# Turning gathered rows with DMA transposes of 16-bit planes in place of TensorE, in an FFT filter with a mixture of experts

## The chip, the cores and the metric

The kernel runs on one core of a Trainium2 chip. The metric is device time in microseconds (us) of one execution, the median of the runs shown. The engines are called as in the profile: PE (TensorE matmuls), PEld (its weight loads), DVE (VectorE), ACT (ScalarE), POOL (GpSimd) and SP (SyncE, which only issues DMAs here).

## The reference

A spectral filter over each of 8 sequences of 2496 rows of 256, then a mixture of 8 experts, each row going to the two experts with the highest noisy logits:

```python
X = np.fft.rfft(x, axis=1)
y = np.fft.irfft(X * (filt_r + 1j * filt_i)[None], n=2496, axis=1)
x = y.reshape(19968, 256)
logits = x @ w_gate
noisy = logits + np.log1p(np.exp(x @ w_noise)) * noise
top2 = np.argpartition(-noisy, 2, axis=1)[:, :2]      # then a softmax over the two: top2_w
out = np.zeros((19968, 256))
for e in range(8):
    for k in range(2):
        mask = top2[:, k] == e
        h = np.maximum(x[mask] @ w1[e], 0.0)           # w1[e] is 256 x 1024
        out[mask] += top2_w[mask, k, None] * (h @ w2[e])
```

## The kernel before

**Precision.** Every large product is made of three matmuls: each fp32 operand is split into a rounded high part (a cast on ACT, name ending in `h`) and the rest (a subtraction on DVE, ending in `l`), and `_mm3` adds high x high, low x high and high x low (L121 to L123).

**Two streams.** The FFT is a stream of small steps over the 8 sequences ("sets"): matrix products of 39 and 64 points, then the gate's logits and top two, then lists of rows for each expert, written to `lst`; the filtered rows with their gate values go to `y` in memory. The experts' stream works on blocks. A block is up to 512 rows of one expert: set 0 gives 2 blocks, set 1 ten; later sets give pairs of blocks of one expert (parts i = 0 and 1, which share the weights), the end has single blocks, then blocks of 256 and 128 rows. 71 blocks have 512 rows. `run` mixes the streams: after each of the 13 places of a block (`yield`) it takes as many FFT steps of later sets as `PACE` allows: the number of steps times the set's length in places may not exceed the places done times `PACE[i]`, 200 for the second set. In front of a weight change at a set's start `FILL` may add steps, and PE's instructions of the turn are then pinned behind them. The engines' orders come from a scheduler at build time; a pin (`after`, `pin`) fixes one instruction behind another.

**A block.** `fetch` keeps up to two blocks ahead. `gather` issues for each tile of 128 rows an indirect DMA from POOL (L993) into a slot of `stage` (8 slots `xg` of 264 columns: 256 values, 8 gates). `front` loads the expert's weights through SP (`load_w`, L1030) and splits them (`wsplit`, L1058, L1059). `turn` brings rows to columns: for each half `kc` of the 256 values four PE transposes of 128x128 (L1009) fill one PSUM bank `xps`, ACT casts it to `mxh` (L1013), DVE makes `mxl` (L1014); POOL copies the block's gate column to `gt` (L1018). Then, for each eighth f of the 1024 hidden values, six matmuls into an `hps` bank (of every three, two have the tag `hps` and the third shares `yps`), ACT's `hh` (relu, L1096) and DVE's `hl` (L1097), with w2's casts between where the weights are new. Last, for each of four row tiles t, eight times a 512-column and a 256-column matmul (L1121, L1122) into one of two `yps` banks, ACT's `o` (times the gate, L1126), DVE's sum of the second half (L1128), and POOL's indirect DMA that adds the rows to `out` (L1129). The next block's `turn` is called between h and y, so that the scheduler may place it beside the y matmuls.

Of the kernel before, what the change touches and what calls it, by code (L numbers as in the profile page):

```python
# [11 lines left out]
R32 = mybir.dt.float32r  # L12
F16 = mybir.dt.float16
I32 = mybir.dt.int32
AF = mybir.ActivationFunctionType
ALU = mybir.AluOpType
AX = mybir.AxisListType
# [5 lines left out]
NG = 22  # L23
# [103 lines left out]
    return ap.bitcast(F32)  # L127


PACE = {0: 110, 1: 200, 2: 40}  # L130
PACES = 115
FILL = {0: 0, 1: 14}
RAW = 3
# [8 lines left out]
class Moe:  # L142
# [39 lines left out]
    def setup(self):  # L182
# [12 lines left out]
        self.sgn = cp.tile([64, 20], F32, name="sgn")  # L195


        self.stage = cp.tile([128, 2048 + 8 * YW + 1536], F32, name="stage")
# [252 lines left out]
    def logits(self, r):  # L451
        nc, P = self.nc, self.P
        if r == 0:
            self.uh = P.tile([120, 24, 16], R32, name="uh")
# [262 lines left out]
    def gate(self, bt, lgp):  # L717
# [30 lines left out]

        m, c, oh = [], [], []
        for i in range(2):  # L750
            mi, ci, oi = t(f"m{i}", [RP, NG]), t(f"c{i}", [RP, NG]), t(f"oh{i}")
# [213 lines left out]
        nc.gpsimd.tensor_copy(ids, t)  # L965
        return ids, n, nt, s, self.tabs[i]

    def front(self, blk, xg, fill=None):


        nc = self.nc
        lt, n, nt, s, tabi, ready = blk
        with self.after(self.spw):
            re = nc.sync.value_load(tabi[0:1, 1, s:s + 1], min_val=0, max_val=E - 1)
        self.ra = nc.gpsimd.value_load(tabi[0:1, 1, s:s + 1], min_val=0, max_val=E - 1)
        w1st = self.load_w(re, "w1", nt)
        w1 = [self.wsplit(w1st[q], "w1", q) for q in range(4)]
        w2st = self.load_w(re, "w2", nt)
        if fill:
            fill()  # L980
        if fill and self.held_any:
            xT = self.pin(self.turn, xg, nt, hold=False, only=[self.nc.tensor.engine])
        else:
            xT = self.turn(xg, nt)
        return w1, xT, w2st

    def gather(self, blk, i):

        lt, n, nt, s, tabi, ready = blk
        xg = []  # L990
        for t in range(nt):
            x = self.slot("xg")
            self.pin(lambda: self.nc.gpsimd.indirect_dma_start(  # L993
                out=x, out_offset=None, in_=self.y[:BLK + ready * ROWS],
                in_offset=bass.IndirectOffsetOnAxis(ap=lt[:, i, t:t + 1], axis=0)),
                hold=False, only=[self.nc.gpsimd.engine])
            xg.append(x)
        return xg, self.turns["xg"] + 1 - nt

    def turn(self, xg, nt):  # L1000

        nc, P = self.nc, self.P
        xT = []
        xg, at = xg
        w = 128 * nt
        for kc in range(2):
            q = self.PS.tile([128, 512], F32, name="xps", bufs=1)
            for t in range(nt):
                nc.tensor.transpose(q[:, t * 128:(t + 1) * 128], xg[t][:, kc * 128:(kc + 1) * 128], self.ident)  # L1009
# [3 lines left out]
            nc.scalar.copy(h, q[:, :w])  # L1013
            nc.vector.tensor_sub(l, q[:, :w], f32v(h))  # L1014
            xT.append((h, l))
        gate = P.tile([128, 4, 1], F32, name="gt", bufs=3)[:, :nt]
        rows = self.stage[:, 2048:2048 + 8 * YW].rearrange("p (s w) -> p s w", w=YW)[:, at:at + nt, D:]
        nc.gpsimd.tensor_copy(gate, rows[:, :, bass.ds(self.ra, 1)])  # L1018
        xT.append(gate)
        return xT  # L1020

    def load_w(self, re, nm, nt):
# [39 lines left out]
    def fetch(self, may):  # L1062

        if len(self.ahead) < 2 and may():
            p = next(self.parts, None)
            if p is not None:
                self.ahead.append((*p, self.gather(*p)))

    def expert(self, parts, may, fill=None):

        nc, P = self.nc, self.P
        self.parts, self.ahead = parts, []
        self.fetch(lambda: True)
        cur = None
        while self.ahead:
            blk, i, xg = self.ahead.pop(0)
            lt, n, nt, s, tabi, ready = blk
            w = 128 * nt
            if cur is None:
                cur = self.front(blk, xg, fill)  # L1080
# [4 lines left out]
            self.fetch(may)  # L1085
            hh = []
            for f in range(8):

                p = self.PS.tile([128, 512], F32, name="hps", tag="hps" if f % 3 < 2 else "yps", bufs=2)[:, :w]
                for kc in range(2):  # L1090
                    wh, wl = w1[f // 2]
                    o = (f % 2) * 128
                    _mm3(nc, p, wh[:, kc, o:o + 128], wl[:, kc, o:o + 128], *xT[kc], start=(kc == 0), stop=(kc == 1))
                h = P.tile([128, 512], R32, name="hh", bufs=8)[:, :w]
                l = P.tile([128, 512], R32, name="hl", bufs=8)[:, :w]
                nc.scalar.activation(h, p, AF.Relu)  # L1096
                nc.vector.scalar_tensor_tensor(l, p, 0.0, f32v(h), op0=ALU.max, op1=ALU.subtract)  # L1097
                hh.append((h, l))
                if f % 2 and i == 0:
                    w2.append(self.wsplit(w2st[f // 2], "w2", f // 2))  # L1100
                yield
            late = not self.ahead
            if late:
                self.fetch(lambda: True)
            if self.ahead:
                b2, i2, x2 = self.ahead[0]
                cur = (w1, self.turn(x2, nt), None) if i2 else self.front(b2, x2, fill if late else None)
            self.fetch(may)
            yield
            for t in range(nt):  # L1110

# [14 lines left out]
                nc.scalar.activation(o, p, AF.Copy, scale=gate[:, t])  # L1126
                if wide:
                    nc.vector.scalar_tensor_tensor(o, bank[:, 1], gate[:, t], o, op0=ALU.mult, op1=ALU.add)  # L1128
                a = nc.gpsimd.indirect_dma_start(  # L1129
# [116 lines left out]
```

## Time and profile before

| | |
|---|---|
| median of 3 runs | 2316.27 us (2315.95 to 2317.04) |
| profiled execution | 2308.6 us, span 2306.8 us |
| PE busy | 2253.9 us, 98% |
| DVE busy | 1540.0 us, 67% |
| ACT busy | 1183.1 us, 51% |
| POOL busy | 925.5 us, 40% |
| mean granted TensorE clock | 0.993 of full speed |
| DMA | 328.58 MB, 142 GB/s over the span |

Busy time counts each engine alone. Matmuls overlap their neighbours in the records (a 512-column matmul is shown with 0.39 to 0.40 us while the next starts 0.23 us after it), so a PE near 100% says that PE did not wait. What an edit is worth is read from the waits, the chain that ended last, and the distance from one start to the next. The profiled execution is 7.7 us shorter than the median of the runs.

### The profile page before, as it was taken

The numbers are of one execution on the slowest core, as the hardware profiler recorded it, in microseconds if no ns is written. First come the engines' busy times: TensorE is split into PE (matmuls) and PEld (weight loads), VectorE is DVE, ScalarE is ACT, GpSimd is POOL, SyncE is SP. The second block draws the span as 40 slices with busy tenths as digits, with TensorE's granted clock in tenths as the row PEclk, the third lists the DMA queues.
The fourth block names the chain that finished last, engine by engine and source line by source line (L and its number), as shares of the span: only waits on it lengthen the run. The fifth ranks groups of instructions, "written<-read, shape, count | busy, mean of one in ns | idle before, by whom it ended". The sixth has DMA issues, their size and how long they took to land.

```text
span 2306.8 us, 39164 instructions
## 1 busy us (share of the span) xinstructions
PE 2253.9 (98%) x13023; PEld 1888.2 (82%) x13023; DVE 1540.0 (67%) x3348; ACT 1183.1 (51%) x2369; POOL 925.5 (40%) x819
## 2 busy tenths in 40 slices
PE   8889999999999999999999999999999999999998
PEld 5448888888788888888888888888888888889997
DVE  4767797687669765875659655964444445557886
ACT  6655655654554554444544444444344444546775
POOL 4014253343334333443344433435454544444442
PEclk9989999999999999999999999999999999999999
DMA  8686757755655555454544553444444444657774
GB/s 239 178 255 188 199 141 195 177 149 135 171 137 126 140 140 129 103 144 118 118 114 106 137 142 85 91 99 89 96 92 91 90 98 105 149 138 233 218 215 130
DMA packets 283957, 328.58 MB, mean 142 GB/s; under 512 B 37243, under 2 KB 196963, under 8 KB 283747
## 3 DMA queue, kind: packets, MB, share of 16 engines
q1 hardware_dynamic: 222435, 241.60, 34.5%
q0 software_dynamic: 61312, 84.40, 21.6%
q8 instruction: 104, 1.70, 0.3%
q14 instruction: 106, 0.87, 0.1%
HBM read 221.44 MB, written 105.25 MB: 142 GB/s over the span
## 4 chain that ended last, share of the span: by engine, by line
PE 89%; DMA 4%; DVE 3%; ACT 2%; issue 1%; SPq 1%; POOL 0%; POOLq 0%; ACTq 0%; DVEq 0%
PE yps L1121 21%; PE hps L121 12%; PE hps L122 12%; PE hps L123 12%; PE yps L1122 10%; PE xps L1009 3%; PE q L428 2%; PE yps L123 2%; PE yps L121 2%; PE yps L122 2%; PE q L492 1%; PE u L439 1%; DMA stage<-w 1%; DMA x<-x 1%; PE q L317 1%
## 5 line engine op out<-in xcount | busy, mean ns | idle before, releaser
L1121 PE MATMUL yps<-w,hh 128*128 128x512 f32 x2080 | 737.6, 399 | 0.6 <-DVE stage L1128 0.6
L1129 POOL DMA_INDIRECT out<-stage,ids x316 | 524.8, 1661 | 291.2 <-DVE stage L1128 116.9
L993 POOL DMA_INDIRECT stage<-y,ids x316 | 324.0, 1025 | 623.7 <-PE xps L1009 247.1
L1122 PE MATMUL yps<-w,hl 128*128 128x256 f32 x2080 | 563.3, 280 | 0.1
L1097 DVE SCALAR_TENSOR_TENSOR hl<-hps,hh 128x512 fp32r<-128x512 f32 (+2 forms) x712 | 435.0, 626 | 153.7 <-ACT hh L1096 151.9
L122 PE MATMUL hps<-mxl,w1h 128*128 128x512 f32 (+2 forms) x1424 | 533.0, 375 | 0.0
L121 PE MATMUL hps<-mxh,w1h 128*128 128x512 f32 (+2 forms) x1424 | 524.1, 378 | 1.7 <-DVE hl L1097 1.4
L123 PE MATMUL hps<-mxh,w1l 128*128 128x512 f32 (+2 forms) x1424 | 525.0, 370 | 0.0
L1096 ACT ACTIVATE hh<-hps 128x512 fp32r<-128x512 f32 (+2 forms) x712 | 377.7, 550 | 247.2 <-PE hps L123 241.7
L1121 PEld LDWEIGHTS yps<-w,hh 128*128 128x128 f32 x2080 | 384.2, 188 | 80.4 <-DVE stage L1128 0.9
L1122 PEld LDWEIGHTS yps<-w,hl 128*128 128x128 f32 x2080 | 391.1, 188 | 19.9 <-DVE mxl L1014 1.2
L121 PEld LDWEIGHTS hps<-mxh,w1h 128*128 128x128 f32 x1424 | 265.1, 188 | 50.5 <-DVE hl L1097 3.7
L123 PEld LDWEIGHTS hps<-mxh,w1l 128*128 128x128 f32 x1424 | 268.4, 188 | 45.5
L122 PEld LDWEIGHTS hps<-mxl,w1h 128*128 128x128 f32 x1424 | 268.3, 188 | 40.4 <-issue 0.2
L1126 ACT ACTIVATE stage<-yps,gt 128x256 f32<-128x256 f32 x316 | 142.3, 476 | 281.1 <-PE yps L1122 256.7
L1128 DVE SCALAR_TENSOR_TENSOR stage<-yps,gt,stage 128x256 f32<-128x256 f32 x260 | 119.4, 479 | 184.5 <-ACT stage L1126 184.1
L1014 DVE TENSOR_TENSOR mxl<-xps,mxh 128x512 fp32r<-128x512 f32 (+2 forms) x178 | 112.1, 630 | 149.1 <-ACT mxh L1013 147.0
L1013 ACT CAST mxh<-xps 128x512 fp32r<-128x512 f32 (+2 forms) x178 | 95.9, 539 | 203.3 <-PE xps L1009 170.3
L1058 ACT CAST w1h<-stage 128x512 fp32r<-128x512 f32 x180 | 111.8, 621 | 99.8 <-PE hps L122 52.1
L1059 DVE TENSOR_TENSOR w1l<-stage,w1h 128x512 fp32r<-128x512 f32 x180 | 123.7, 687 | 55.5 <-ACT w1h L1058 54.6
L965 POOL CAST ids<-lt 128x8 int32<-128x8 f32 (+3 forms) x63 | 16.2, 257 | 336.2 <-DMA lt<-lst 330.1
L1059 DVE TENSOR_TENSOR w<-stage,w 128x512 fp32r<-128x512 f32 x216 | 142.4, 686 | 7.9 <-ACT w L1058 7.4
(222 smaller groups left out, 3082.4 us busy)
## 6 DMA issues: line engine op xcount, KB each, us to landing
stage<-w SPq DMA_DIRECT2D x396, 256.0 KB
x<-x SPq DMA_DIRECT2D x88, 256.0 KB
fd<-c SPq DMA_DIRECT2D x77, 240.0 KB
wb<-w SPq DMA_DIRECT2D x18, 1024.0 KB
fx<-fd SPq DMA_DIRECT2D x140, 128.0 KB
out<-z SPq DMA_DIRECT2D x24, 702.0 KB
y<-yt SPq DMA_DIRECT2D x40, 248.6 KB
y<-yt SPq DMA_DIRECT2D x40, 234.0 KB
```

Of the source, the lines that this page charges most:

```text
L121: nc.tensor.matmul(o, lh, rh, start=start, stop=False)
L122: nc.tensor.matmul(o, lh, rl, start=False, stop=False)
L123: nc.tensor.matmul(o, ll, rh, start=False, stop=stop)
L993: self.pin(lambda: self.nc.gpsimd.indirect_dma_start(out=x, out_offset=None, in_=self.y[:BLK + ready * ROWS], in_offset=bass.IndirectOffse ...
L1059: nc.vector.tensor_sub(l, sv, f32v(h))
L1096: nc.scalar.activation(h, p, AF.Relu)
L1097: nc.vector.scalar_tensor_tensor(l, p, 0.0, f32v(h), op0=ALU.max, op1=ALU.subtract)
L1121: nc.tensor.matmul(bank, h, hl, start=(f == 0), stop=False)
L1122: nc.tensor.matmul(p, l, hl[:, 0], start=False, stop=(f == 7))
L1126: nc.scalar.activation(o, p, AF.Copy, scale=gate[:, t])
L1128: nc.vector.scalar_tensor_tensor(o, bank[:, 1], gate[:, t], o, op0=ALU.mult, op1=ALU.add)
L1129: a = nc.gpsimd.indirect_dma_start(out=self.io["out"][:BLK + ready * ROWS], out_offset=bass.IndirectOffsetOnAxis(ap=ids[:, t:t + 1], axis= ...
```

## The change

A block of 512 rows from the second set on (`by_dma`: 4 tiles and `ready` over 1) is turned without PE. For each two of its row tiles ACT copies the rows' fp32 values as 16-bit halves into two planes, all low halves and then all high halves of a row (`flip`, 128x1024 elements of 16 bits; the buffer `pl` has one slot for two tiles). SP then issues for each of the two tiles a DMA transpose of 128 x 512 16-bit values (128 KB) into `xt`, which has one buffer for a whole block. `turn` has DVE interleave the two planes of a half `kc` again into fp32 columns (128 x 1024 elements of 16 bits into `x32`, one slot), pinned behind the last `hl` of the block before; ACT's cast and DVE's subtraction read `x32` in SBUF instead of PSUM. 69 blocks go this way: 138 plane copies on ACT, 276 DMA transposes on SP, 138 copies on DVE, and 552 PE transposes fewer.

The first plane copy of a block is called in the h phase two turns ahead (after f = 4), the second after its predecessor's turn; both are pinned behind an activation. To make room, `xg` has 4 slots instead of 8 and `yo` 4 instead of 6. For such blocks the third bank of the h loop is `xps` (now free, one buffer) instead of `yps`. The gate copy is made when the planes are begun. `PACE` of the second set is 225. Two smaller tiles share buffers (`uh`, `oh`).

```diff
-PACE = {0: 110, 1: 200, 2: 40}
+PACE = {0: 110, 1: 225, 2: 40}
...
-        at, n, w = {"wst": (0, 4, 512), "xg": (2048, 8, YW), "yo": (2048 + 8 * YW, 6, 256)}[nm]
+        at, n, w = {"wst": (0, 4, 512), "xg": (2048, 4, YW), "yo": (2048 + 4 * YW, 4, 256),
+                    "x32": (3072 + 4 * YW, 1, 512), "pl": (3584 + 4 * YW, 1, 512)}[nm]
...
-        if fill and self.held_any:
-            xT = self.pin(self.turn, xg, nt, hold=False, only=[self.nc.tensor.engine])
+        if fill and self.held_any and ent[3] is None:
+            xT = self.pin(self.turn, ent, hold=False, only=[self.nc.tensor.engine])
...
+    def flip(self, late=None):
+
+        if self.turning is None:
+            ent = next((e for e in self.ahead if e[3] is None), None)
+            if self.standing or ent is None or not self.by_dma(ent[0]):
+                return
+            self.standing = True
+            xt = self.P.tile([128, 4, 512], U16, name="xt", bufs=1)
+            ent[3] = xt, self.take(ent)
+            self.turning, self.turned = ent, 0
+        ent, at = self.turning, self.turning[2][1]
+        xt, t = ent[3][0], self.turned
+        pl = self.slot("pl").bitcast(U16).rearrange("p (t two d) -> p t two d", t=2, two=2)
+        rows = self.held_rows(at + t, 2)[:, :, :D].bitcast(U16).rearrange("p t (d two) -> p t two d", two=2)
+        with self.after(late):
+            self.nc.scalar.copy(pl, rows)
+        for k in range(2):
+            self.nc.sync.dma_start_transpose(xt[:, :, 128 * (t + k):128 * (t + k) + 128], pl[:, k].rearrange("p two d -> p (two d)"))
+        self.turned += 2
+        if self.turned == 4:
+            self.turning = None
+
+    def by_dma(self, blk):
+        return blk[2] == BLK // 128 and blk[5] > 1
...
         for kc in range(2):
-            q = self.PS.tile([128, 512], F32, name="xps", bufs=1)
-            for t in range(nt):
-                nc.tensor.transpose(q[:, t * 128:(t + 1) * 128], xg[t][:, kc * 128:(kc + 1) * 128], self.ident)
+            if ent[3]:
+                q = self.slot("x32")
+                with self.after(self.lastl):
+                    nc.vector.tensor_copy(q.bitcast(U16).rearrange("p (t two) -> p two t", two=2), ent[3][0][:, kc::2])
+            else:
+                q = self.PS.tile([128, 512], F32, name="xps", bufs=1)
+                for t in range(nt):
+                    nc.tensor.transpose(q[:, t * 128:(t + 1) * 128], xg[t][:, kc * 128:(kc + 1) * 128], self.ident)
...
+            while self.turning or any(a[3] is None and self.by_dma(a[0]) for a in self.ahead):
+                self.flip(e)
+            if not self.ahead or self.by_dma(self.ahead[0][0]) or nt < BLK // 128:
+                self.fetch(may)
+            third = ("xps", 1) if ent[3] else ("yps", 2)
...
-                p = self.PS.tile([128, 512], F32, name="hps", tag="hps" if f % 3 < 2 else "yps", bufs=2)[:, :w]
+                tag, bufs = ("hps", 2) if f % 3 < 2 else third
+                p = self.PS.tile([128, 512], F32, name="hps", tag=tag, bufs=bufs)[:, :w]
...
+                if f == 4:
+                    self.flip(e)
                 yield
             late = not self.ahead
             if late:
                 self.fetch(lambda: True)
+                self.flip()
...
             self.fetch(may)
+            self.flip()
             yield
```

The order of the instructions moves with it. In the rows below a name is the tile written, an arrow, and the tiles read. First PE at the end of a block in the part of the program that has no FFT work left; `mxh_18925` is the next block, and the last h matmul of the block that ends stands 14 rows above the first one shown. Before:

```order
L1121 MATMUL yps<-w_18658,hh 128x512
L1122 MATMUL yps<-w_18658,hl 128x256
L1121 MATMUL yps<-w_18683,hh 128x512 x2
L1122 MATMUL yps<-w_18683,hl 128x256 x2
L121 MATMUL hps<-mxh_18925,w1h 128x512
L1009 MATMUL xps<-ident,stage 128x128 x4
L122 MATMUL hps<-mxl_18926,w1h 128x512
L123 MATMUL hps<-mxh_18925,w1l 128x512
```

After, from the last h matmul of a block (`mxh_19323`) on; `mxh_19556` is the next block:

```order
L124 MATMUL hps<-mxh_19323,w1l 128x512
L1180 MATMUL yps<-w_19527,hl 128x256 x2
L1179 MATMUL yps<-w_19527,hh 128x512 x2
L1180 MATMUL yps<-w_19527,hl 128x256 x2
L1179 MATMUL yps<-w_19552,hh 128x512 x2
L1180 MATMUL yps<-w_19552,hl 128x256 x2
L1179 MATMUL yps<-w_19552,hh 128x512 x2
L1180 MATMUL yps<-w_19552,hl 128x256 x2
L122 MATMUL hps<-mxh_19556,w1h 128x512 x3
L123 MATMUL hps<-mxl_19557,w1h 128x512
```

The transposes between the h and y matmuls are gone, and fourteen y matmuls of two row tiles stand between the last h matmul of one block and the first of the next, which opens three banks at once.

ACT at the same kind of place. Before, the casts of the next block (`mxh`) stand among the last activations of h (L1096), ahead of the y tiles' `o` (L1126):

```order
L1058 CAST w_20036<-stage 128x512
L1096 ACTIVATE hh<-hps 128x512 x5
L1013 CAST mxh_20044<-xps 128x512
L1096 ACTIVATE hh<-hps 128x512
L1013 CAST mxh_20053<-xps 128x512
L1126 ACTIVATE stage<-yps,gt 128x256 x2
```

After (L1030 is the plane copy, L1150 `hh`, L1061 `mxh`, L1184 `o`):

```order
L1150 ACTIVATE hh<-hps 128x512 x3
L1030 COPY stage<-stage 128x1024
L1150 ACTIVATE hh<-hps 128x512 x5
L1061 CAST mxh_19556<-stage 128x512
L1184 ACTIVATE stage<-yps,gt 128x256 x2
L1061 CAST mxh_19561<-stage 128x512
L1184 ACTIVATE stage<-yps,gt 128x256 x2
L1030 COPY stage<-stage 128x1024
L1150 ACTIVATE hh<-hps 128x512
```

The casts have moved behind the last activation of h, one plane copy stands inside the h phase, and the other between the last `o` and the next block's first `hh`.

DVE after, at the end of that block (L1151 is `hl`, L1053 the interleaving copy, L1062 `mxl`, L1186 the y tiles' sum):

```order
L1151 SCALAR_TENSOR_TENSOR hl<-hps,hh 128x512 x8
L1053 COPY stage<-xt 128x2x512
L1062 TENSOR_TENSOR mxl_19557<-stage,mxh_19556 128x512
L1186 SCALAR_TENSOR_TENSOR stage<-yps,gt,stage 128x256 x2
L1053 COPY stage<-xt 128x2x512
L1062 TENSOR_TENSOR mxl_19562<-stage,mxh_19561 128x512
```

Both copies stand behind all eight `hl` of the block before, the second behind the sums of its first two y tiles too.

More of the change, by code (lines that the diff above doesn't have):

```diff
@@ L14 @@
 I32 = mybir.dt.int32
+U16 = mybir.dt.uint16
 AF = mybir.ActivationFunctionType
@@ L195, in setup @@
         self.sgn = cp.tile([64, 20], F32, name="sgn")
-        self.stage = cp.tile([128, 2048 + 8 * YW + 1536], F32, name="stage")
+        self.stage = cp.tile([128, 2048 + 4 * YW + 2048], F32, name="stage")
         self.turns = {}
@@ L453, in logits @@
         if r == 0:
-            self.uh = P.tile([120, 24, 16], R32, name="uh")
+            self.uh = P.tile([120, 24, 16], R32, name="uh", tag="ut0", bufs=1)
             self.ul = P.tile([120, 24, 16], R32, name="ul")
@@ L750, in gate @@
         for i in range(2):
-            mi, ci, oi = t(f"m{i}", [RP, NG]), t(f"c{i}", [RP, NG]), t(f"oh{i}")
+            mi, ci = t(f"m{i}", [RP, NG]), t(f"c{i}", [RP, NG])
+            oi = P.tile(sh, F32, name=f"oh{i}", tag=("gl", "oh1")[i], bufs=1)
             v.tensor_reduce(mi, nz, axis=AX.X, op=ALU.max)
@@ L980, in front @@
             fill()
-        if fill and self.held_any:
-            xT = self.pin(self.turn, xg, nt, hold=False, only=[self.nc.tensor.engine])
+        if fill and self.held_any and ent[3] is None:
+            xT = self.pin(self.turn, ent, hold=False, only=[self.nc.tensor.engine])
         else:
-            xT = self.turn(xg, nt)
+            xT = self.turn(ent)
         return w1, xT, w2st
     def gather(self, blk, i):
+        nc = self.nc
         lt, n, nt, s, tabi, ready = blk
+        if i == 0:
+            self.ra = nc.gpsimd.value_load(tabi[0:1, 1, s:s + 1], min_val=0, max_val=E - 1)
         xg = []
@@ L992, in gather @@
             x = self.slot("xg")
-            self.pin(lambda: self.nc.gpsimd.indirect_dma_start(
+            self.pin(lambda: nc.gpsimd.indirect_dma_start(
                 out=x, out_offset=None, in_=self.y[:BLK + ready * ROWS],
                 in_offset=bass.IndirectOffsetOnAxis(ap=lt[:, i, t:t + 1], axis=0)),
-                hold=False, only=[self.nc.gpsimd.engine])
+                hold=False, only=[nc.gpsimd.engine])
             xg.append(x)
-        return xg, self.turns["xg"] + 1 - nt
@@ L1000, in turn, with held_rows, take @@
-    def turn(self, xg, nt):
+        return xg, self.turns["xg"] + 1 - nt, self.ra
+    def held_rows(self, at, n):
+        return self.stage[:, 2048:2048 + 4 * YW].rearrange("p (s w) -> p s w", w=YW)[:, at:at + n]
+    def take(self, ent):
+        xg, at, ra = ent[2]
+        gate = self.P.tile([128, 4, 1], F32, name="gt", bufs=3)[:, :len(xg)]
+        self.nc.gpsimd.tensor_copy(gate, self.held_rows(at, len(xg))[:, :, D:][:, :, bass.ds(ra, 1)])
+        return gate
+    def flip(self, late=None):
[18 more added lines that the diff above has]
+            self.turning = None
@@ L1015, in turn @@
             xT.append((h, l))
[L1016 to L1019, printed above, removed]
+        self.standing = self.standing and ent[3] is None
+        xT.append(ent[3][1] if ent[3] else self.take(ent))
+        ent[3] = ent[3] or ()
         return xT
@@ L1066, in fetch @@
             if p is not None:
-                self.ahead.append((*p, self.gather(*p)))
+                self.ahead.append([*p, self.gather(*p), None])
     def expert(self, parts, may, fill=None):
         nc, P = self.nc, self.P
-        self.parts, self.ahead = parts, []
+        self.parts, self.ahead, self.turning, self.standing, self.lastl = parts, [], None, False, None
         self.fetch(lambda: True)
+        self.flip()
         cur = None
         while self.ahead:
-            blk, i, xg = self.ahead.pop(0)
+            ent = self.ahead.pop(0)
+            blk, i = ent[:2]
             lt, n, nt, s, tabi, ready = blk
@@ L1079, in expert @@
             if cur is None:
-                cur = self.front(blk, xg, fill)
+                cur = self.front(ent, fill)
             w1, xT, w2st = cur
@@ L1104, in expert @@
                 self.fetch(lambda: True)
+                self.flip()
             if self.ahead:
-                b2, i2, x2 = self.ahead[0]
-                cur = (w1, self.turn(x2, nt), None) if i2 else self.front(b2, x2, fill if late else None)
+                e2 = self.ahead[0]
+                cur = (w1, self.turn(e2), None) if e2[1] else self.front(e2, fill if late else None)
             self.fetch(may)
+            self.flip()
             yield
```

17 lines of the change are left out of this document (9 added, 8 removed).

## The prediction

> **What bounds the kernel now.** I read the page first (busy shares, then the chain of waits), next the busy time in windows of 100 us, then the groups of instructions with their shapes apart, and last the timeline at one turn of a block and the DMA and wait lists.
>
> From the page of the kernel before, the busy shares, the DMA queue of SP, and the chain by engine and by line:
>
> ```profile
> PE 2253.9 (98%) x13023; PEld 1888.2 (82%) x13023; DVE 1540.0 (67%) x3348; ACT 1183.1 (51%) x2369; POOL 925.5 (40%) x819
> q1 hardware_dynamic: 222435, 241.60, 34.5%
> PE 89%; DMA 4%; DVE 3%; ACT 2%; issue 1%; SPq 1%; POOL 0%; POOLq 0%; ACTq 0%; DVEq 0%
> PE yps L1121 21%; PE hps L121 12%; PE hps L122 12%; PE hps L123 12%; PE yps L1122 10%; PE xps L1009 3%; PE q L428 2%; PE yps L123 2%; PE yps L121 2%; PE yps L122 2%; PE q L492 1%; PE u L439 1%; DMA stage<-w 1%; DMA x<-x 1%; PE q L317 1%
> ```
>
> TensorE sets the end: 89% of the chain is PE, and its row transposes (L1009) are 3% of 2306.8 us, 69 us. DVE and ACT have room on average, SP's queue moves 57 ns per packet (34.5% of 16 x 2306.8 us over 222435).
>
> The windows, by stage (window, PE busy, PEld, DVE, ACT, POOL, clock, DMA share, GB/s):
>
> ```profile
> 500.00:600.00 100.00, 92.65 (x617) 81.54 (x619) 72.57 (x176) 44.88 (x91) 39.59 (x30) 0.98 0.55 140
> 1200.00:1300.00 100.00, 99.36 (x562) 83.08 (x562) 83.69 (x221) 46.69 (x91) 46.80 (x39) 1.00 0.52 120
> 1700.00:1800.00 100.00, 100.00 (x522) 84.58 (x521) 48.05 (x80) 42.63 (x81) 48.22 (x43) 1.00 0.43 93
> ```
>
> From 200 us on PE is never free, with one hole of 7 us at 500 to 600 where the first sets hand over. So any microsecond taken off PE comes off the end, and any new wait of PE goes straight onto it: there is no slack in which either could vanish. Up to about 1430 us FFT work stands between the blocks and can cover a wait; from 1530 to 2100 us there is nothing but blocks.
>
> **What is removed: 552 transposes of PE.** The group, with two rows of the shapes it feeds, and the timeline around one of its fours:
>
> ```profile
> L1009 PE MATMUL xps<-ident,stage 128*128 128x128 f32 x632 | 101.5, 274 | 14.2 <-DMA stage<-y,ids 12.7 <-DVE mxl L1014 1.4
> L1013 ACT CAST mxh<-xps 128x512 fp32r<-128x512 f32 x142 | 83.4, 587 | 189.2 <-PE xps L1009 161.3 <-PE hps L123 25.9 <-DVE st L857 0.5
> L1014 DVE TENSOR_TENSOR mxl<-xps,mxh 128x512 fp32r<-128x512 f32 x142 | 97.9, 690 | 141.7 <-ACT mxh L1013 141.1
> ...
> 1509.76 0.39 PE L123 MATMUL hps<-mxh,w1l 128*128 128x512 f32 x1
> 1509.98 0.60 PE L1009 MATMUL xps<-ident,stage 128*128 128x128 f32 x4
> 1510.42 0.27 PE L929 MATMUL ra<-ident,rx 128*56 128x128 f32 x1
> ```
>
> Four transposes hold PE from 1509.98 to 1510.42, 0.11 us each; the chain's 69 us over 632 says the same. 552 x 0.109 = **-60 us**, or 0.87 us for each of the 69 blocks of 512 rows. (Busy time would say 552 x 101.5/632 = 89 us, but overlaps count twice there.) The 14.2 us in which PE waited ahead of transposes are 12.7 us of late gathers, 5 times; the first rows of a set now have a longer way (two copies and a DMA more), so I book nothing for them and keep 14 us either way for the range.
>
> **What is added: ACT and DVE.** 138 plane copies on ACT and 138 re-interleaving copies on DVE, 1024 elements per lane each. No such copy stands in the trace; the rows to price them by:
>
> ```profile
> L1096 ACT ACTIVATE hh<-hps 128x512 fp32r<-128x512 f32 x568 | 329.7, 597 | 228.1 <-PE hps L123 222.6 <-DVE oc L917 1.0 <-DVE off L871 0.8
> L1096 ACT ACTIVATE hh<-hps 128x256 fp32r<-128x256 f32 x112 | 40.1, 387 | 13.3 <-PE hps L123 13.3
> L1097 DVE SCALAR_TENSOR_TENSOR hl<-hps,hh 128x512 fp32r<-128x512 f32 x568 | 382.2, 686 | 142.9 <-ACT hh L1096 141.1 <-PE yps L1122 0.5
> L1097 DVE SCALAR_TENSOR_TENSOR hl<-hps,hh 128x256 fp32r<-128x256 f32 x112 | 44.5, 418 | 7.3 <-ACT hh L1096 7.3
> L919 DVE TENSOR_TENSOR oc<-half,lo 117x512 f16<-117x512 f16 x88 | 53.4, 617 | 0.0
> L917 DVE TENSOR_TENSOR oc<-half,hi 117x224 f16<-117x224 f16 x88 | 30.1, 354 | 3.4 <-PE ra L922 2.9 <-DVE rx L926 0.2
> ```
>
> ACT: 256 elements more cost 210 ns, so 1024 cost 597 + 420 = 1.02 us, together 140 us (51% to 58%). DVE: by L1097 686 + 536 = 1.22 us; by the 16-bit rows 288 elements cost 263 ns, so 617 + 468 = 1.09. I take 1.15, together 159 us (67% to 74%). Bounds: 0.69 us if 1024 16-bit elements run like 512 of 32 bits, 2.3 us if the step of two elements on the 16-bit side costs double. Off the path both totals cost nothing, PE's 98% covers them. What counts is where one copy stands in a chain that PE waits for.
>
> **Place one, the end of a block.** The next block's rows used to come through PSUM half a block early. Now DVE's copy is held behind the block's last `hl`, so PE's next block waits for last h matmul, `hh`, `hl`, copy, `mxh`. Durations: the matmul's last 0.17 us (0.40 long, 0.23 to its successor), 0.60, 0.69, 1.15, 0.59, and four hand-overs of 0.04 (last two rows below: 1513.51 + 0.47 to 1514.02), 3.36 us in all.
>
> ```profile
> 1512.85 0.28 PE L1122 MATMUL yps<-w,hl 128*128 128x256 f32 x1
> 1512.96 0.39 PE L1121 MATMUL yps<-w,hh 128*128 128x512 f32 x1
> 1513.19 0.28 PE L1122 MATMUL yps<-w,hl 128*128 128x256 f32 x1
> ...
> 1513.51 0.47 ACT L1126 ACTIVATE stage<-yps,gt 128x256 f32<-128x256 f32 x1 [4.53 <-PE yps L1122]
> ...
> 1514.02 0.49 DVE L1128 SCALAR_TENSOR_TENSOR stage<-yps,gt,stage 128x256 f32<-128x256 f32 x1 [1.79 <-ACT stage L1126]
> ```
>
> A y step is 0.11 + 0.23 us. In the FFT-free stretch the changed order leaves, in 12 of some 28 blocks, eight 256-column and six 512-column steps between the last h matmul and the next block, 2.33 us: 12 x 1.03 = **+12 us**. In the other blocks y tile 2 is put straight behind tiles 0 and 1 (5.07 us of cover, the chain fits), but it takes tile 0's PSUM bank and so waits for ACT's 0.476 and DVE's 0.479 on it:
>
> ```profile
> L1126 ACT ACTIVATE stage<-yps,gt 128x256 f32<-128x256 f32 x316 | 142.3, 476 | 281.1 <-PE yps L1122 256.7
> L1128 DVE SCALAR_TENSOR_TENSOR stage<-yps,gt,stage 128x256 f32<-128x256 f32 x260 | 119.4, 479 | 184.5 <-ACT stage L1126 184.1
> ```
>
> With 0.17 for the matmul's end and two hand-overs that is 1.2 us against 0.1 of PE work, at about 20 places of the new order and at none of the old (smallest distance there 2.6 us): 20 x 1.1 = **+22 us**. In the FFT stretch five blocks are short of 3.4 us by 2 us in all.
>
> **Place two, the head of a block.** The second plane copy stands on ACT between the last `o` of a block and `hh` 0 of the next. Where no w2 cast stands there too, PE needs `hh` 0 some 2.1 us after the last y matmul and gets it at 2.5 to 2.8 (0.17 + 0.48 + 1.02 + 0.60 and hand-overs): 11 blocks x 0.5 = **+6 us**. With the w2 cast PE has 3.5 us, and the chain 3.1.
>
> **The DMAs: 276 transposes of 128 KB on SP's queue.** They come in pairs, and none is in this trace. Plain 128 KB loads in the chain, with SP's issue, and what SP's queue waits for:
>
> ```profile
> 60.69 0.64 SPq L368
> 61.38 3.08 DMA fx<-fd
> 458.07 1.52 SPq L368
> 572.87 4.52 DMA fx<-fd
> ...
> SPq L1030 <- DVE w1l L1059: 535.1, 136, 19.1
> ```
>
> The first pair of a block can start once DVE's second copy has freed `xt`, about 5.5 us after the last h matmul: 3.36 to the end of the first cast, 0.69 for `mxl`, 1.15 for the second copy (the 512-column buffer between has one slot), hand-overs, and at times a y step of 0.48 on DVE between. The second plane copy wants the plane buffer back at 10.4 to 11.7 us (three y tiles and three half-banks of the next block, plus `o`). So up to **about 5 us for a pair cost nothing**; beyond that ACT stands, `hh` 0 behind it, and PE with it, in all 69 blocks. Bounds: two issues of 0.64 and one landing of 3.08, 4.4 us; or one after the other, slowly, 2 x (1.52 + 4.52) = 12.1 us. A 128 KB transpose is nearest to a 128 KB load and two on one queue overlap, so I take 4.4 to 5 and nothing. SP works in order: weight loads queue behind the transposes, but they are needed a block later, and SP's 535 us of waits for `w1l` show that slots, not SP, hold them.
>
> [...]
>
> **The rest at nothing.** The h loop's third bank comes from `xps` instead of `yps`: PE's 512-column rows cover its eviction as before. POOL's counts stay; gathers start a block earlier, from four slots instead of eight. 225 instead of 200 steps moves the hole at 500 to 600 us (7.35 us of idle): 0, with 5 us either way.
>
> Sum: -60 + 12 + 22 + 2 + 6 = **-18 us**. The profiled execution took 2308.6 us (span 2306.8 and 1.8 around it) and would take about 2290; the median of the runs shown, 2316.27, lies 7.7 higher, so **2298 us**.
>
> **Rivals.**
> - *The waits are hidden.* If the copies run at 0.69 us (the chain 2.9) and PE's queue finds the banks free, only the 60 us count, with the early gathers' 14 at most: 2242 to 2275. For it: in the FFT stretch, some 40 of the 69 blocks, the order leaves next to no shortfall. Against: place one's bank wait rests on rows that are in the trace.
> - *The stalls eat the gain:* 8 us more at each place, 2312 to 2321, no change.
> - *Strided 16-bit copies cost double.* DVE 2.3 us: the end chain becomes 4.5, 2.2 us short in 12 late blocks and 14 us in the early ones, +26 over the forecast; ACT 2.04 us: 0.7 us in the blocks with a w2 cast and 1.0 in the 11 without, some +40. About 2364. It decides from 1.4 us a copy. Against: 16-bit rows here cost what 32-bit ones do.
> - *The transposes do not overlap.* A pair at 2 x (1.52 + 3.08) = 9.2 us is 4.2 over the limit in each of 69 blocks: +290, about 2590. It decides at 5 us, and each microsecond more is 69. For it: the 4.4 us bound is close to 5, and a 16-bit row of 128 elements is 256 bytes, 1024 packets for a pair, which at 57 ns over 16 engines are 3.6 us without issue or latency. Against: the two pairs of a block have the time of its 48 h matmuls and 32 y steps, 22 us at 0.23 and 0.34 us. [...]
>
> That the change does not do what it says is excluded by the order: the transposes and copies stand in it.
>
> **Chances.** Forecast (2275 to 2312) 0.40, waits hidden 0.13, no change 0.11, double copies 0.14, slow transposes 0.22. About 0.2%, 4.6 us, can be told from no change here: faster 0.53, same 0.11, slower 0.36. The forecast's own range is 2275 to 2312; both signs hold much, so the range for eight in ten is 2250 to 2385: it takes in the hidden waits and the double copies, and leaves out the slow transposes beyond 6.3 us for a pair.
>
> **What would show it.** PE's L1009 group at 80 to 100 with 9 us in the chain. In the windows from 1530 to 2100 PE at about 96% instead of 100, its idle time put down to `mxh`'s chain (DVE copy, ACT cast) and to `o` of y tile 0 (L1186), about 1 us a time. Copies at 1.0 and 1.15 us. A transpose pair from issue to landing under 5 us, and ACT's second plane copy not waiting for it. If ACT's plane copies wait on DMA for microseconds in every block, or `hh` follows them late, the forecast is wrong on the slow side; if PE stays at 100% late, on the fast side.

## The result

The changed kernel takes 2382.73 us (median, 2374.54 to 2385.71) against 2316.11 before: ratio 1.028, 95% interval 1.0265 to 1.0294. It is slower by 66.6 us where 18 us less were forecast. The profiled execution has a span of 2372.8 us, 66.0 more than before.

The page after, busy shares, DMA queue of SP and the chain:

```profile
PE 2248.0 (95%) x12471; PEld 1837.0 (77%) x12471; DVE 1626.5 (69%) x3486; ACT 1310.6 (55%) x2507; POOL 939.3 (40%) x819
q1 hardware_dynamic: 372579, 277.81, 42.9%
PE 66%; DMA 10%; DVE 10%; ACT 7%; issue 5%; SPq 2%; POOL 0%; ACTq 0%; DVEq 0%; POOLq 0%
PE yps L1179 16%; PE hps L122 10%; PE hps L123 9%; PE hps L124 9%; PE yps L1180 8%; DMA xt<-stage 5%; PE q L430 2%; ACT stage L1030 1%; DVE hl L1151 1%; ACT hh L1150 1%; PE yps L122 1%; PE yps L124 1%; PE yps L123 1%; PE q L494 1%; DMA stage<-w 1%
```

PE fell from 89% of the chain to 66%. DMA has 10%, half of it the transposes (`xt<-stage`), and DVE and ACT together 17% where they had 5%. The chain that ended last now runs through three other resources for a quarter of the time.

The same windows as before (window, PE, PEld, DVE, ACT, POOL, clock, DMA share, GB/s):

```profile
500.00:600.00 100.00, 94.14 (x611) 81.50 (x610) 84.20 (x209) 54.15 (x104) 36.59 (x27) 1.00 0.71 164
1200.00:1300.00 100.00, 93.98 (x526) 75.63 (x525) 73.33 (x154) 51.97 (x99) 44.09 (x36) 1.00 0.62 136
1700.00:1800.00 100.00, 96.51 (x468) 78.05 (x467) 52.15 (x86) 49.07 (x86) 49.74 (x44) 1.00 0.62 119
```

The late window is what I forecast (96% of PE). The middle one isn't: 94% where PE had been at 99%, in a stretch where FFT work was to cover everything.

A busy share is too kind here, since records of matmuls overlap (one of 512 columns is 0.40 us long). The starts tell more: I took from each PE start to the next the usual distance for that matmul (0.23 us for 512 columns, 0.11 for 128) and added up what exceeds it by over 0.12 us. After 200 us PE stood for 25 us before and 131 after, by stage:

| stage, us | PE stands, before | after |
|---|---|---|
| 200 to 600 | 15.0 | 31.0 |
| 600 to 1000 | 3.3 | 29.4 |
| 1000 to 1500 | 5.4 | 27.9 |
| 1500 to 2100 | 0.4 | 31.8 |
| 2100 to the end | 0.7 | 10.5 |

That is +106 us, of which 60 are paid for by the transposes. Another part of the 66 is clock. After 170 us and up to the end of the work, the clock record shows PE at half clock for 3.4 us before and for 34 us after; half of the difference, an estimated 15 us, is lost. The two overlap: at half clock a 512-column matmul takes 0.43 us to the next start, so some 10 of the 106 are counted in those stretches already. -60 + 96 + 15 = +51 of the +66; the rest lies in distances that are longer by less than 0.12 us.

What ACT, DVE and PE wait for now, from the list of waits (us in total, times, longest):

```profile
DVE hl L1151 <- ACT hh L1150: 247.5, 166, 6.0
ACT stage L1030 <- DMA xt<-stage: 195.7, 74, 8.0
ACT mxh L1061 <- DVE stage L1053: 101.7, 69, 5.4
PE yps L1179 <- DVE stage L1186: 21.0, 22, 1.1
PE yps L1179 <- ACT hh L1150: 13.6, 19, 2.8
PE yps L122 <- ACT hh L1150: 11.3, 6, 3.3
```

L1030 is the plane copy. It stood for transposes 74 times out of 138, 2.6 us each. The last two lines are PE at y matmuls (L122 in the first blocks) whose `hh` ACT had not made yet; before, the one such line has 1.1 us. One place where the plane copy stood, ACT and SP in the part without FFT work (start, duration, instruction, wait ahead of it):

```profile
1699.81 0.48 ACT L1184 ACTIVATE stage<-yps,gt 128x256 f32<-128x256 f32 x1
1700.19 1.03 ACT L1030 COPY stage<-stage 128x1024 uint16<-128x1024 uint16 x1
...
1701.64 1.09 ACT L1150 ACTIVATE hh<-hps 128x512 fp32r<-128x512 f32 x2
1703.29 0.60 ACT L1150 ACTIVATE hh<-hps 128x512 fp32r<-128x512 f32 x1 [0.56 <-PE hps L124]
1707.20 1.05 ACT L1030 COPY stage<-stage 128x1024 uint16<-128x1024 uint16 x1 [3.31 <-DMA xt<-stage]
1708.15 1.08 ACT L1150 ACTIVATE hh<-hps 128x512 fp32r<-128x512 f32 x2
```

```profile
1701.24 2.61 SPq L1032 DMA_TRANSPOSE xt<-stage  x2
```

The second plane copy of a block ends at 1701.22 and SP issues its two transposes at once, 1.3 us each. Three `hh` later, at 1703.89, ACT has come to the first plane copy of the next block. It needs the one plane buffer, which these transposes are still reading, and stands until 1707.20, with the next `hh` behind it.

### The profile page after: what moved, and what is told of

It reads as the page before. It is cut to its first block, busy times and chain, and to the rows that moved or that the text cites. A ratio compares the mean times of both kernels' runs of the same rounds, so it can differ in the third digit from the quotient of the medians.

```text
span 2372.8 us, 38598 instructions
## 1 busy us (share of the span) xinstructions
PE 2248.0 (95%) x12471; PEld 1837.0 (77%) x12471; DVE 1626.5 (69%) x3486; ACT 1310.6 (55%) x2507; POOL 939.3 (40%) x819
## 3 DMA queue, kind: packets, MB, share of 16 engines
q1 hardware_dynamic: 372579, 277.81, 42.9%
## 4 chain that ended last, share of the span: by engine, by line
PE 66%; DMA 10%; DVE 10%; ACT 7%; issue 5%; SPq 2%; POOL 0%; ACTq 0%; DVEq 0%; POOLq 0%
PE yps L1179 16%; PE hps L122 10%; PE hps L123 9%; PE hps L124 9%; PE yps L1180 8%; DMA xt<-stage 5%; PE q L430 2%; ACT stage L1030 1%; DVE hl L1151 1%; ACT hh L1150 1%; PE yps L122 1%; PE yps L124 1%; PE yps L123 1%; PE q L494 1%; DMA stage<-w 1%
## 5 line engine op out<-in xcount | busy, mean ns | idle before, releaser
L1187 POOL DMA_INDIRECT out<-stage,ids x316 | 543.2, 1719 | 582.1 <-DVE stage L1186 349.1
L1179 PE MATMUL yps<-w,hh 128*128 128x512 f32 x2080 | 731.2, 402 | 35.2 <-DVE stage L1186 21.0
L1151 DVE SCALAR_TENSOR_TENSOR hl<-hps,hh 128x512 fp32r<-128x512 f32 (+2 forms) x712 | 432.1, 624 | 252.0 <-ACT hh L1150 247.5
L122 PE MATMUL hps<-mxh,w1h 128*128 128x512 f32 (+2 forms) x1424 | 518.4, 384 | 21.6 <-ACT mxh L1061 9.2
L1180 PE MATMUL yps<-w,hl 128*128 128x256 f32 x2080 | 533.9, 283 | 1.4 <-DVE hl L1151 1.3
L124 PE MATMUL hps<-mxh,w1l 128*128 128x512 f32 (+2 forms) x1424 | 527.3, 371 | 0.0
L1179 PEld LDWEIGHTS yps<-w,hh 128*128 128x128 f32 x2080 | 371.5, 189 | 114.7 <-DVE stage L1186 25.0
L1150 ACT ACTIVATE hh<-hps 128x512 fp32r<-128x512 f32 (+2 forms) x712 | 374.2, 550 | 142.4 <-PE hps L124 138.2
L122 PEld LDWEIGHTS hps<-mxh,w1h 128*128 128x128 f32 x1424 | 262.1, 189 | 94.5 <-DVE hl L1151 31.4
L124 PEld LDWEIGHTS hps<-mxh,w1l 128*128 128x128 f32 x1424 | 269.3, 189 | 46.8
L1184 ACT ACTIVATE stage<-yps,gt 128x256 f32<-128x256 f32 x316 | 141.2, 473 | 224.0 <-PE yps L1180 154.9
L1030 ACT COPY stage<-stage 128x1024 uint16<-128x1024 uint16 x138 | 143.9, 1043 | 209.3 <-DMA xt<-stage 195.7
L1186 DVE SCALAR_TENSOR_TENSOR stage<-yps,gt,stage 128x256 f32<-128x256 f32 x260 | 119.5, 479 | 119.9 <-ACT stage L1184 119.2
L1106 DVE TENSOR_TENSOR w<-stage,w 128x512 fp32r<-128x512 f32 x216 | 147.7, 690 | 59.1 <-ACT w L1105 54.0
L1061 ACT CAST mxh<-stage 128x512 fp32r<-128x512 f32 x138 | 85.7, 621 | 119.3 <-DVE stage L1053 101.7
L1105 ACT CAST w<-stage 128x512 fp32r<-128x512 f32 x216 | 133.2, 621 | 30.7 <-issue 13.4
```

The source lines that it names most:

```text
L122: nc.tensor.matmul(o, lh, rh, start=start, stop=False)
L124: nc.tensor.matmul(o, ll, rh, start=False, stop=stop)
L1030: self.nc.scalar.copy(pl, rows)
L1105: nc.scalar.copy(h, sv)
L1106: nc.vector.tensor_sub(l, sv, f32v(h))
L1150: e = nc.scalar.activation(h, p, AF.Relu)
```

## The experiments

All ratios are to runs of the kernel before on the same chip. A gain or loss against the changed kernel is taken between the two ratios, times 2316 us.

**e1: no transposes.** ACT's copy writes `xt` itself.

```diff
-        pl = self.slot("pl").bitcast(U16).rearrange("p (t two d) -> p t two d", t=2, two=2)
...
-            self.nc.scalar.copy(pl, rows)
-        for k in range(2):
-            self.nc.sync.dma_start_transpose(xt[:, :, 128 * (t + k):128 * (t + k) + 128], pl[:, k].rearrange("p two d -> p (two d)"))
+            self.nc.scalar.copy(xt[:, :, 128 * t:128 * t + 256].rearrange("p (two a) b -> p two a b", two=2), rows.rearrange("p t two d -> p two t d"))
```

> Left out: the DMA transposes; ACT writes its plane copy straight into xt in another order, so the blocks' rows are scrambled, while every copy, cast, matmul and buffer stays (pl is not used). Theory A (ACT stands in its order behind the transposes, 196 us in 74 of 138 plane copies, and hh, the FFT's copies and PE behind it): ACT's wait for DMA is gone, and 30 to 50 us come back, 2330 to 2350 us. Rival B (the new order's own waits, y tile 2 behind its PSUM bank and the copy chain at a block's end, make up the loss): 2370 to 2383, with PE's waits for L1186 and for mxh as long as now.

2329.88 us, ratio 1.0067 (1.0045 to 1.009): 49 us less than the change. Theory A holds for most of the loss, and ACT's wait for transposes can't be told here from the transposes themselves (e5 does that). But with 60 us of PE work gone and no transpose at all it is still 15 us slower than before, so something else takes some 75 us. PE stands 94 us after 200 us here, 27 of them from 1500 to 2100.

**e2: no block by DMA.**

```diff
-        return blk[2] == BLK // 128 and blk[5] > 1
+        return False
```

> The changed kernel with no block turned by DMA: only the smaller row and output buffers (4 slots each instead of 8 and 6), PACE 225 and the shared tiles are left of the change. If the smaller buffers are a part of the loss (the 256-row blocks, which are not turned by DMA, take 12.45 instead of 11.92 us each in the changed kernel): 2325 to 2345. If the loss is all in the DMA path: 2312 to 2320.

2357.36 us, 1.0182 (1.0162 to 1.0201), above both expectations. With four row slots and PE as the reader, gathers come late: 37 us at PE's transposes in the list of waits of this run, against 12.7 before.

```profile
PE xps L1057 <- DMA stage<-y,ids: 37.1, 33, 3.9
```

In the changed kernel that wait is 5.7 us, since the plane copies free the slots a block earlier. So these 43 us are no part of its 66 as they stand. What both share is the end: the 256-row blocks take 12.45 us from one to the next, as in the change, and 11.92 before. 13 such blocks are 7 us.

**e3: only the last 17 full blocks by DMA.**

```diff
-        return blk[2] == BLK // 128 and blk[5] > 1
+        return blk[2] == BLK // 128 and blk[5] == NB
```

> Only the last 17 full blocks go by DMA (those whose rows are all ready), the other 52 through TensorE. By the late blocks of the two traces (23.95 instead of 23.15 us each) 17 cost 14 us, and what the smaller buffers cost is in it too. Theory A, loss mostly in the FFT stretch: at most 20 us over the kernel with no block by DMA. Rival C, the loss is the same for every block (66/69 us): 16 us over it.

2360.17 us, 1.0192 (1.017 to 1.0213): the same as e2. 17 blocks by DMA among those without FFT work neither gain nor lose against PE turning from four slots. It does not tell theory A from rival C, since e2 was no clean base.

**e4: PACE 225 in the kernel before.**

```diff
-PACE = {0: 110, 1: 200, 2: 40}
+PACE = {0: 110, 1: 225, 2: 40}
```

> The kernel before with PACE of the second set 225 instead of 200, one line. If the pace is no part of the loss: 2311 to 2321. If it makes the first sets collide: over 2325.

2314.41 us, 0.9999 (0.9989 to 1.0009): in the kernel before, the pace costs nothing.

**e5: the first plane copy behind the last hh.** The scheduler had been free to put it three `hh` behind the second one, and e5 pins it behind the last `hh` (at both calls between h and y). The description of the change says that both plane copies are pinned; its diff shows that these two calls, `self.flip()`, give nothing to pin behind, and from the third block of a run of such blocks on the first copy comes from there.

```diff
-            self.flip()
+            self.flip(e)
```

> The first plane copy of a block, which the scheduler puts three activations behind the second one of the block before, is pinned behind the last hh. By the trace it stood there for the transposes of the pair before (1 to 5 us, 74 times, 196 us). Theory A (ACT's stand in front of the transposes costs the time): ACT's wait for DMA falls under 50 us and the kernel to 2335 to 2355 us. Rival B (PE's waits at y tile 2 and at the end chain cost it): not under 2370.

2336.35 us, 1.0103 (1.0086 to 1.012), 41 us less than the change, with every transpose still there. ACT's wait is gone, from the list of waits of this run:

```profile
ACT stage L1030 <- DMA xt<-stage: 14.6, 8, 3.5
```

196 us of ACT's standing fall to 15, and the time follows to within 8 us of the kernel without any transposes. So it is not the transposes' length or their traffic (SP's queue still moves 277.81 MB) that cost these 41 us, but where ACT's instruction that waits for them stands.

**e6: the third h bank from `yps`.**

```diff
-            third = ("xps", 1) if ent[3] else ("yps", 2)
+            third = ("yps", 2)
```

> The third h bank comes from yps again. Rival B: PE's 45 us in front of y tile 2 fall under 10 and the kernel to 2340 to 2350 us. Theory A, where ACT's late hh hold PE anyway: the wait moves to hh, 2365 to 2383.

2401.86 us, 1.0401 (1.0383 to 1.0418), 28 us more than the change, outside both ranges. The list of waits of this run shows why:

```profile
PE yps L1179 <- ACT hh L1150: 44.6, 31, 3.1
PE yps L1179 <- DVE stage L1186: 2.0, 3, 1.0
```

The wait at y tile 2 is gone (21.0 us to 2.0), as rival B had it, but another has grown in its place (13.6 us to 44.6): PE at a block's first y matmuls, waiting for `hh`. That is theory A's wait, longer than A had expected. At one such place ACT's plane copy starts at 1707.24, after 4.61 us for the transposes, three `hh` follow it, and PE stands until 1708.83. From 1500 to 2100 PE now stands 64 us instead of 32, 40 of them at these matmuls. This window of this run, then of the change:

```profile
1500.00:2100.00 600.00, 557.77 (x2676) 457.69 (x2675) 304.57 (x498) 280.69 (x496) 254.09 (x227) 0.98 0.55 112
```

```profile
1500.00:2100.00 600.00, 577.59 (x2814) 469.40 (x2812) 322.26 (x523) 297.96 (x524) 273.15 (x238) 1.00 0.60 120
```

So the wait at y tile 2 does go with the third bank from `xps`, but without that bank PE comes to wait longer for the `hh` behind ACT's stand. The clock takes a part too: 58 us at half clock from 170 us on, against 34.

**e7: the interleaving copies not pinned.**

```diff
-                with self.after(self.lastl):
+                with self.after(None):
```

> DVE's interleaving copies are no longer pinned behind the last hl. Rival B: the first copy runs in the h phase, the wait of PE's next block for mxh (about 35 us over the run) falls under 15, 2350 to 2365 us. Theory A: xt is free earlier too, so the transposes start earlier, but ACT's place in front of them stays: 2360 to 2383.

2324.03 us, 1.0066 (1.0045 to 1.0087), 50 us less than the change, more than either expectation. The same window of this run:

```profile
1500.00:2100.00 600.00, 597.93 (x3012) 498.13 (x3010) 344.85 (x635) 309.25 (x563) 285.33 (x252) 1.00 0.63 133
```

PE stands 4.8 us there instead of 31.8: the wait for `mxh` is gone there (5.6 us before this edit), and the one at y tile 2 as well (18.8 us to 0.4). One pin had made both. With the copy early, the next block's h matmuls can stand between the y tiles again, as before the change; with the copy behind the last `hl` there was nothing else to put there, and tile 2 followed tiles 0 and 1 directly. ACT still stands 149 us for transposes in this run, but 46 us less.

**e8: e5, e6 and e7 together.**

> The three edits together: plane copy behind the last hh, third bank from yps, copies not pinned. If the three waits add up (some 35, 40 and 20 us): 2280 to 2300 us, faster than before. If they stand in for one another: 2320 to 2345.

2322.31 us, 1.0045 (1.0028 to 1.0062). They do not add up, and e6's edit is a loss here too: e9, which leaves it out, has a ratio of 0.9986.

**e9: e5 and e7.**

> The changed kernel with the first plane copy pinned behind the last hh (as e5) and the interleaving copies not pinned (as e7); the third bank stays xps. If what is left in e7 is ACT's stand in front of the transposes (149 us of wait there): 2300 to 2312 us. If the waits of the FFT stretch come from elsewhere (DVE's copies stand for xt instead, the smaller row buffers): 2318 to 2330.

2311.45 us, 0.9986 (0.9975 to 0.9998): 68 us less than the change, and back at the time before. PE stands 2.1 us from 1500 to 2100. From 200 to 1500 it still stands 71 us (24 before), and 44 us are at half clock, 31 of them in one stretch at 608 us. DVE's early copies now stand in front of transposes, half of the time in the FFT stretch and half behind it:

```profile
DVE stage L1053 <- DMA xt<-stage: 75.3, 37, 3.9
```

Behind the FFT this costs PE nothing that can be seen (2.1 us), and from 590 to 645 us, around the long stretch at half clock, DVE stands for transposes only once, 3.1 us. All of the 7.6 us that ACT's plane copies wait for them in this run fall there too. How much of the FFT stretch's loss is the copies, and how much the smaller buffers, was not separated.

**e10 and e11: the last 17 and the last 27 full blocks by DMA, with the buffers of before.** Both have the pins of e9 (on the plane copies at the calls between h and y, none on the interleaving copies), 8 row slots, 6 output slots, rows fetched as early as before, and PACE 200. The planes and `x32` lie over row slots 4 to 7, and `xt` over an FFT buffer. At the borders between the two kinds of blocks some rows are overwritten before they are turned, so a few blocks' values are wrong; every instruction is there.

```diff
-        return blk[2] == BLK // 128 and blk[5] > 1
+        return blk[2] == BLK // 128 and blk[5] == NB       # e11: blk[5] >= NB - 1
...
-            xt = self.P.tile([128, 4, 512], U16, name="xt", bufs=1)
+            xt = self.P.tile([128, 8, 512], U16, name="xt", tag="G", bufs=2)[:, :4]
```

> The kernel before in all buffers (8 row slots, 6 output slots, PACE 200), and only the last 17 full blocks by DMA, with the two pins of e9; their x32 and plane buffers lie over the upper four row slots, xt over an FFT buffer. No FFT work is left there and SP's queue is half empty. If PE's 0.87 us a block come out whole: 15 us, 2297 to 2303 us, faster than before. If each block's waits eat them: 2308 to 2318.

> As e10, from one set earlier on: 27 blocks, ten of them beside the FFT's last steps. If FFT work covers the waits as my prediction had it: 23 us, 2289 to 2296 us. If the DMA path loses beside FFT work (theory A's stretch, where the blocks by DMA lost about 1 us each): between e10 and before, 2303 to 2316.

e10: 2307.37 us, 0.996 (0.9944 to 0.9976). e11: 2301.27 us, 0.9939 (0.9924 to 0.9955). Both are faster than before, by 9 and 14 us, six tenths of what PE's work alone is worth (17 and 27 x 0.87); as far as the intervals tell, the ten blocks ahead of the last set help about as much each as the others.

**e12: e11 with planes, `xt` and interleaved rows in one FFT buffer**, so that row slots stay whole and each block has its own plane buffer.

```diff
-        pl = self.slot("pl").bitcast(U16).rearrange("p (t two d) -> p t two d", t=2, two=2)
+        pl = xt[:, 4:6].rearrange("p t (two d) -> p t two d", two=2)
...
-                q = self.slot("x32")
-                with self.after(self.lastl):
-                    nc.vector.tensor_copy(q.bitcast(U16).rearrange("p (t two) -> p two t", two=2), ent[3][0][:, kc::2])
+                q = ent[3][0][:, 6:8].rearrange("p a b -> p (a b)")
+                nc.vector.tensor_copy(q.rearrange("p (t two) -> p two t", two=2), ent[3][0][:, kc:4:2])
+                q = q.bitcast(F32)
```

> As e11, but xt, the planes and the interleaved rows of a block lie together in one of the FFT's two large buffers, so that the row slots stay whole and a block's planes no longer share a slot with the next block's. By e11's blocks (22.3 instead of 23.15 us each where nothing waits) 27 blocks are worth 23 us, of which e11 kept 13. If what it lost was the overlaid slots: 2292 to 2298 us. If it was the border of the last two sets: 2298 to 2305. Under 2306 either way, faster than both kernels.

2288.79 us, 0.9924 (0.991 to 0.9937), faster than both kernels: 18 us under the kernel before, which took 2306.15 on this chip, and three quarters of 27 x 0.87. On the chip of e11 the ratio gives 2297, 4 us under e11; the two intervals overlap, so that the overlaid slots cost e11 time is likely and not shown. Its windows (as above) and its copy groups:

```profile
600.00:1500.00 900.00, 899.06 (x4951) 746.24 (x4951) 612.66 (x1267) 443.63 (x856) 363.92 (x312) 1.00 0.53 126
1500.00:2100.00 600.00, 596.63 (x3097) 500.09 (x3096) 370.88 (x751) 318.12 (x586) 285.36 (x253) 1.00 0.65 137
...
L1028 ACT COPY xt<-stage 128x1024 uint16<-128x1024 uint16 x54 | 56.5, 1047 | 5.6 <-DVE mxl L1060 3.4 <-PE q L493 2.2
L1050 DVE COPY xt<-xt 128x1024 uint16<-128x1024 uint16 x54 | 40.6, 753 | 45.5 <-DMA xt<-xt 42.7 <-DMA stage<-w 2.7
```

ACT's plane copies wait for no transpose (5.6 us in all, none of it DMA). DVE stands 43 us for them, but PE does not: 4.8 us from 1500 to 2100. Most pairs of blocks there follow at 44.5 us, where they took 46.3: 0.89 us a block, so the 0.87 of its eight transposes come out whole except at a few borders.

## Why the prediction was wrong, step by step

**The work removed: right.** 552 transposes left PE, and e12's pairs show 0.89 us a block where nothing takes their place.

**The copies: ACT's right in size, DVE's too dear.** The groups of the changed kernel, from the view with shapes apart:

```profile
L1030 ACT COPY stage<-stage 128x1024 uint16<-128x1024 uint16 x138 | 143.9, 1043 | 209.3 <-DMA xt<-stage 195.7 <-DMA stage<-y,ids 7.9 <-issue 4.1
L1053 DVE COPY stage<-xt 128x1024 uint16<-128x1024 uint16 x138 | 104.1, 755 | 3.0 <-DMA xt<-stage 2.1
```

ACT's 1.04 us stood as 1.02. DVE's 0.755 lies near the lower bound (0.69), not at the 1.15 that I took; the rival of double cost is out.

**The pair of transposes: the length right, its price wrong.** This is the step that failed. I took 4.4 to 5 us for a pair. Measured from the first issue to the last packet, the median pair took 4.2 us (3.3 to 6.9 for 9 in 10), and a transpose is issued every 1.26 us:

```profile
L1032 SPq DMA_TRANSPOSE xt<-stage x276: 1188/1261/7205, 198.5 to 2110.8; - x138
```

"Up to about 5 us for a pair cost nothing" was worked out for the first pair alone, which the second plane copy waits for. The second pair has a reader too: the plane buffer has one slot, and the next block's first plane copy is put three `hh` behind the second one, 2.7 us after it in the piece shown. The order quoted ahead of the prediction has both places (`hh` x3 and then L1030 inside the h phase; L1030 and then `hh` between two blocks), and I counted only what a plane copy delays by its own 1.02 us, not what it waits for. What I had named as a sign of being wrong, ACT's plane copies waiting for DMA and `hh` following late, is what the trace shows, in 74 of 138 copies. e5 moves that one instruction, keeps the transposes, and gets 41 of the 66 us back. In the piece shown ACT works in order: one `hh` ends at 1703.89, and the next, whose last matmul had ended at 1705.10 (PE's row of L124: 1704.71 + 0.39), starts at 1708.15, behind a copy that it has nothing to do with. SP works in order too: from 698.41 us it stood 15.43 us in front of a transpose and issued nothing else. The rival with slow transposes named the right queue (ACT, then `hh`, then PE) with the wrong cause: nothing was slow, at 4.2 us a pair. The loop of "22 us" that spoke against it was no argument, since ACT stood at its own place in the loop, 74 times for 2.6 us, not at the loop's average.

**The end of a block and y tile 2: right without FFT work, far too little beside it.** From 1500 to 2100 PE stood 18.8 us at y tile 2, in 16 places of 1.2 us (forecast 22, some 20 places of 1.1), and 5.6 us for the next block's `mxh`, in 10 places of 0.6 us (forecast 12, in 12 places of 1.03). One of the 16:

```profile
1691.74 0.39 PE L1180 MATMUL yps<-w,hl 128*128 128x256 f32 x2
1693.16 0.50 PE L1179 MATMUL yps<-w,hh 128*128 128x512 f32 x1 [1.02 <-DVE stage L1186]
```

Another 8 us there, waits mostly under 0.5 us for `hh` at a block's first y matmuls and for `hl` ahead of h matmuls, were in no term. From 200 to 1500 us, where I had booked 2 us, the two waits cost 4.4 and 6.5, and a third that I had not seen cost more than both: at y matmuls PE stood 26 us for `hh` (before, 1.5). I counted there how much PE work the order leaves between two instructions, and took the other engines to be on time. ACT was not. And I priced these waits as two; e7 shows one cause, the pin.

**The rest at nothing: wrong for the buffers.** PACE is worth nothing in the kernel before (e4). The four row slots and four output slots together cost about 7 us at the 256-row blocks, which are not turned by DMA; with PE as the reader of all rows the kernel is 43 us slower (e2). e12 with the slots of before has 11.93 us a block at the end.

**FFT cover: wrong.** "In the FFT stretch five blocks are short of 3.4 us by 2 us in all" made that stretch the safe one. It lost most: 64 of the 106 us of standing lie between 200 and 1500 us. In e9, with both pins, the 43rd full block still starts at 1427 us, 20 later than before (1407), though 40 blocks ahead of it have 0.87 us of PE work less each, 35 us (5 us more of the FFT's work are done by then); the full blocks behind it win the 20 back. e12 gets its gain from blocks in or behind the FFT's last steps. Here FFT work is not only cover: ACT, DVE and SP serve it too, and a plane copy that stands on ACT holds the FFT's copies as well as `hh`: one starts at 1334.44, after 7.97 us for transposes, and the FFT's `G` (L431) only behind it, at 1335.39. The smaller buffers are a rival for a part of this loss, and no run has e9's pins with the buffers of before in this stretch: in e2, where no row goes by DMA, the same block starts at 1428 us, against 1410 in e4 and 1414 in e10, which have the buffers of before.

**The sum.** The 66 us are not one cause: e5 gives back 41, e7 50, both 68. They overlap, since e7 alone also shortens ACT's stand (196 us to 149) and PE's wait for `hh` at the y matmuls of L1179 (13.6 us to 3.6). What the smaller buffers and DVE's stand for `xt` still take in e9 is open.

## What to carry to other kernels

Where a step is moved to a DMA with a single buffer, look up for each buffer's next writer where it stands in its engine's order: here ACT stood 196 us in front of the plane buffer with `hh` queued behind it, though a pair of transposes takes 4.2 us. The order that is printed shows this before any run, if one asks of each new instruction what it waits for and not only how long it takes. A pin that looks like one late instruction can take away what another engine would have put in between (e7 gave back 50 us), and a change that wins in one stage and loses in another is worth limiting to that stage, as e12's 18 us show.

## What was not expected of the hardware

**The clock after a wait.** All eight half-clock stretches of the changed kernel from 170 us to the end of the work begin within 2 us of a wait of PE of 1.3 to 3.4 us. Around one of them, PE's rows and then the windows:

```profile
735.15 0.63 PE L1179 MATMUL yps<-w,hh 128*128 128x512 f32 x2
737.79 0.26 PE L925 MATMUL ra<-oc 117*128 117x56 f16 x4 [2.01 <-DVE oc L921]
```

```profile
735.00:739.00 4.00, 1.99 (x18) 1.30 (x16) 4.00 (x9) 0.13 (x1) 0.00 (x0) 1.00 0.04 15
739.00:746.00 7.00, 6.73 (x25) 4.88 (x25) 6.97 (x16) 2.96 (x7) 2.80 (x3) 0.51 0.49 147
746.00:750.00 4.00, 4.00 (x28) 3.35 (x27) 3.93 (x10) 2.28 (x5) 1.50 (x1) 1.00 1.07 204
```

PE waits for 2 us and then runs at 0.51 of the clock for some 7 us. The stretches last 3.4 or 6.8 us in this run, so such a wait costs an estimated 1.7 or 3.4 us more, half of that. But a wait is not always followed by one: of 15 waits over 1.25 us after 200 us eight were not, the longest 2.94 us, up to 217.88; and the 16 waits at y tile 2 from 1500 to 2100 us left the clock at 1.00. What sorts them in this run is where the wait falls. All these stretches begin on one grid of 3.41 us. In eight steps of the grid at full clock PE's rows leave 1.9 to 2.4 us open, and the next step is at half clock each time; no other step leaves over 1.8, since the grid cuts the 2.94 us in two. In the kernel before, from 170 us to the end of the work, the one step with 3.1 us open, at 587 us, is followed by a step at half clock, and two with 1.6 and 1.5 us are not. That the wait causes the half clock is inferred from the order of the two; no run changed a wait alone.

**The packets.** A transpose of 128 x 512 16-bit values moves as 512 packets of 256 bytes, 22 ns each in the mean, where SP's queue had 57 ns a packet before, in packets of 4 to 6144 bytes. By my rival's 57 ns a pair would have needed 3.6 us on the engines; it needed 1.4 (1024 at 22 ns over 16).
